# Pairing different half products on TensorE's two column tiles in the second matrix of an ELU block

## Chip, cores and metric

One Trainium2 chip, one core. The time is that of the device, in microseconds (us), the median of the runs shown. TensorE is called PE, VectorE DVE, ScalarE ACT, GpSimd POOL, as in the profile.

## What is computed

A sketched attention over q, k, v (4 batches, 4 heads, 1088 positions, 32 dimensions) gives an activation x of 4352 rows and 128 columns. An ELU block follows, and it is nearly all of the work:

```
h = x @ w_in                        # 128 -> 2048
g = where(h > 0, h, exp(min(h, 0)) - 1)
out = g @ w_out                     # 2048 -> 128, all float32
```

## The kernel before

The rows of x are worked through in groups of 512 (groups 0 to 7, and a group of 256 at the end). The 2048 columns of h are taken in eight steps of 256, two chunks of 128 partitions each. A step of a group has three parts. PE computes h for 512 rows (`mm1`, four passes of 512 columns per column tile, recorded at L256). ACT and DVE make g of it, chunk by chunk: RELU (L861) and EXP (L863) on ACT, one DVE operation (L869). Two steps later PE multiplies g with w_out (`mm2`).

The order on every engine is written out by hand in one loop: step n issues `mm1` of step n, its ELU, and then the `mm2` of step n-2.

In groups 2 to 7, and in the last two steps of group 1, `mm2` is done in seven half products instead of eight (`mm2_seven`, L770). The step's piece of w_out is a 2x2 of blocks (two chunks, two halves of 64 output features), and g is a 2x2 as well (two chunks, two halves of the 512 rows). Each product takes one 128x64 weight, a block of w_out or one of the sums in SS, and 256 columns, a block of g or one of the sums in tt. POOL makes the sums in tt for each step (`sums7`, L743: L751, then L753, then L754, each needing the one before). The products are called P1 to P7: P1, P2 and P3 need no sum from POOL, P5 and P7 need the result of L751, P6 that of L753 and P4 that of L754.

PE's 128 columns are used as two column tiles of 64 (four of 32 before step 30), each of which writes its own output partitions. Float32 makes two passes of each matrix multiplication. Before, each product runs on both tiles at once with the same weight: 128 of its 256 columns on tile 0 (partitions 0 to 63), the other 128 on tile 64 (partitions 64 to 127). So a step has 7 products x 2 passes of 128 columns on each tile. The products add up in two PSUM banks over the eight steps of a group: pa holds P1, P2, P6 and pb holds P4, P5, P7, P3, 128 columns each. There is one buffer of each, so the next group's first product into a bank waits until the closing additions have read it.

When a group's last `mm2` is through, its closing additions turn the seven sums into four output blocks. ACT copies P2 and P6 out of pa (`fin_seven_copy`, L801). DVE then adds twice from pa (`fin_seven_a`, L815, L816), does the ELU operation of the running step's second chunk, which POOL's next sums wait for, and only then adds three times from pb (`fin_seven_b`, L826 to L828), transposes (L830) and issues the 16 output transfers on the SP queue. In the loop the transposing part stands behind `sums7` of the step.

The 256 rows at the end (`mm1_last`, L903, and `mm2_last`, L924) follow group 7 in 16 short steps. They share four PSUM buffers named h, so `mm1_last` of short step 8 needs the DVE operation of short step 4 (L921) to be over. Group 7's closing additions stand between the DVE operations of short steps 2, 3 and 4.

Of the kernel before, what the change touches and what calls it, by code (L numbers as in the profile page):

```python
# [12 lines left out]
F32 = mybir.dt.float32  # L13
ALU = mybir.AluOpType
U32 = mybir.dt.uint32
MUL, ADD, SUB, MAX = ALU.mult, ALU.add, ALU.subtract, ALU.max
# [6 lines left out]
def _ap(ap: bass.AP, free):  # L23
    return dataclasses.replace(ap, ap=[list(ap.ap[0])] + [list(x) for x in free])
# [3 lines left out]
def kernel(  # L28
# [21 lines left out]
    nc = tc.nc  # L50
    B, H, S, D = q.shape
    R = S1.shape[0]
    P = 128
# [11 lines left out]
    work = ctx.enter_context(tc.tile_pool(name="wk", bufs=2))  # L65
# [91 lines left out]
    W = const.tile([P, NP, 4 * P], F32, name="W")  # L157
# [93 lines left out]
    width = [32]  # L251
# [244 lines left out]
    def half_tile(g, k):  # L496
        return (g // 2, 8 * (g % 2) + k) if g < NQ - 1 else (k, NT - 1)
# [242 lines left out]
    def quarter(g, cp, c, y):  # L740
        return gs[g, cp][:, c].rearrange("p (u x s) -> p u x s", u=2, x=2)[:, :, y, :]

    def sums7(g, cp, c):  # L743
        if c == 0:
            ts[g, cp] = work.tile([P, 4, 2, P], F32, name="tt", tag="raw", bufs=5)
        t = ts[g, cp]
        if c == 0:
            return
        b11, b21 = quarter(g, cp, 0, 0), quarter(g, cp, 1, 0)
        us = [[2 * P, 2], [1, P]]  # L750
        nc.gpsimd.tensor_tensor(_ap(t[:, 0], [[4 * P, 2], [P, 2], [1, P]]), _ap(gs[g, cp][:, 0, P:], [[4 * P, 2]] + us),  # L751
                                _ap(gs[g, cp][:, 0], [[P, 2]] + us), op=SUB)
        nc.gpsimd.tensor_tensor(t[:, 1], t[:, 2], b11, op=ADD)  # L753
        nc.gpsimd.tensor_tensor(t[:, 3], b21, t[:, 1], op=SUB)  # L754
# [13 lines left out]
                                         stop=False, skip_group_check=True, tile_position=(0, r))  # L768

    def mm2_seven(g, cp, first, last):  # L770
        if first and g == 1:
            acc[g].append(psum.tile([P, 512], F32, name="pa", tag="o0", bufs=1))
        elif first:
            acc[g] = [psum.tile([P, 512], F32, name="pa", tag="o0", bufs=1),
                      psum.tile([P, 512], F32, name="pb", tag="o1", bufs=1)]
        a, b = acc[g]
        t, w = ts.pop((g, cp)), [W[:, cp, 2 * P + 64 * i:2 * P + 64 * i + 64] for i in range(4)]
        b11, b21, b22 = quarter(g, cp, 0, 0), quarter(g, cp, 1, 0), quarter(g, cp, 1, 1)
        p1, p2, p6 = (a, 0, w[0], b11), (a, 1, w[2], b21), (a, 2, SS[:, 1, cp], t[:, 1])
        p4, p5 = (b, 0, w[3], t[:, 3]), (b, 1, SS[:, 0, cp], t[:, 0])  # L780
        p7, p3 = (b, 2, SS[:, 2, cp], t[:, 2]), (b, 3, SS[:, 3, cp], b22)
        if g == 1:
            p1, p2, p6, p3 = (b, 0) + p1[2:], (a, 0) + p2[2:], (b, 1) + p6[2:], (a, 1) + p3[2:]
            p5, p7, p4 = (b, 2) + p5[2:], (b, 3) + p7[2:], (a, 2) + p4[2:]
        todo = [p1, p2, p6, p3, p5, p7, p4] if first or last else [p1, p2, p3, p5, p7, p6, p4]
        for i, (bank, col, lhs, rhs) in enumerate(todo):
            for u in range(2):
                for w in range(0, 64, width[0]):
                    r = 64 * u + w
                    nc.tensor.matmul(bank[r:r + width[0], P * col:P * col + P], lhs[:, w:w + width[0]], rhs[:, u],  # L790
                                     start=(first and i in ((0,) if g == 1 else (0, 3))), stop=last, skip_group_check=True,
                                     tile_position=(0, r))
        del gs[g, cp]

    def fin_seven_copy(g):
        a = acc[g][0]
        sa = sas[g] = work.tile([P, 2, P], F32, name="sa", tag="sa", bufs=1)
        if g == 1:
            nc.scalar.copy(sa[:, 0], acc[g][1][:, :P])
            return  # L800
        nc.scalar.copy(sa[:].rearrange("p k s -> p (k s)"), a[:, P:3 * P])  # L801

    def fin_seven_a(g):
        a, sa = acc[g][0], sas.pop(g)
        uu = work.tile([P, 3, P], F32, name="uu", tag="uu", bufs=1)
        cc = work.tile([P, 4, P], F32, name="cc", tag="cc", bufs=1)
        sas[g] = uu, cc
        if g == 1:
            e = acc[g][1][:].rearrange("p (k s) -> p k s", s=P)
            nc.vector.tensor_tensor(uu[:, 0], sa[:, 0], e[:, 1], op=ADD)  # L810
            nc.vector.tensor_tensor(uu[:, 1:], _ap(uu[:, 0], [[0, 2], [1, P]]), e[:, 2:], op=ADD)
            nc.vector.tensor_tensor(cc[:, 3], uu[:, 2], e[:, 2], op=ADD)
            nc.vector.tensor_tensor(cc[:, 0], sa[:, 0], a[:, :P], op=ADD)
            return
        nc.vector.tensor_tensor(uu[:, 0], sa[:, 1], a[:, :P], op=ADD)  # L815
        nc.vector.tensor_tensor(cc[:, 0], sa[:, 0], a[:, :P], op=ADD)  # L816

    def fin_seven_b(g):
        b = acc.pop(g)[0 if g == 1 else 1]
        uu, cc = sas.pop(g)  # L820
        pb = b[:].rearrange("p (k s) -> p k s", s=P)
        if g == 1:
            nc.vector.tensor_tensor(cc[:, 1:3], uu[:, 1:], pb[:, 1:3], op=ADD)
            nc.vector.tensor_tensor(cc[:, 3], cc[:, 3], pb[:, 3], op=ADD)
        else:
            nc.vector.tensor_tensor(uu[:, 1:], _ap(uu[:, 0], [[0, 2], [1, P]]), pb[:, 1:3], op=ADD)  # L826
            nc.vector.tensor_tensor(cc[:, 2:], _ap(uu[:, 2], [[0, 2], [1, P]]), pb[:, 0:2], op=ADD)
            nc.vector.tensor_tensor(cc[:, 1], uu[:, 1], pb[:, 3], op=ADD)  # L828
        ob = work.tile([P, 2, 4, 2, D], F32, name="ob7", tag="ob", bufs=2)
        nc.vector.transpose(ob[:].rearrange("p h k w d -> p (h k w d)"), cc[:].rearrange("p k s -> p (k s)"))  # L830
        rows = out.rearrange("(b w y t) (e l d) -> b w e l y t d", b=B, w=2, t=NT, e=2, l=2)
        for u in range(2):
            bt, t = half_tile(g, 4 * u)
            for lo in range(2):
                r = slice(64 * u + 32 * lo, 64 * u + 32 * lo + 32)
                for hi in range(2):
                    for w in range(2):
                        nc.sync.dma_start(rows[bt, w, hi, lo, :, t:t + 4, :], ob[r, hi, :, w, :])

    def mm1(g, cp, cs=(0, 1)):  # L840
        n = qn[g] * P
# [266 lines left out]
    for n in range(2, N):  # L1108
        g, cp = steps[n]
        mm1(g, cp)  # L1110
        for f, *a in extra.get(n, ()):
            f(*a)
        if n == 30:
            width[0] = 64
        elu(g, cp, 0)
        if seven(g, cp):
            sums7(g, cp, 0)
        for f, *a in extra.get((n, 0), ()):
            f(*a)
        before = steps[n - 2]  # L1120
        ends = n > 3 and seven(*before) and before[1] == NP - 1
        if ends:
            elu_a(g, cp, 1, (0,))
            mm2_seven(*before, False, True)
            fin_seven_copy(before[0])
            elu_a(g, cp, 1, (1,))
            fin_seven_a(before[0])
            if before[0] == 1:
                fin_seven_b(1)
            elu_d(g, cp, 1)  # L1130
        else:
            elu(g, cp, 1)
        if seven(g, cp):
            sums7(g, cp, 1)
        if ends and before[0] > 1:
            fin_seven_b(before[0])
        for f, *a in extra.get((n, 1), ()):
            f(*a)
        g, cp = before
        if seven(g, cp):  # L1140
            if cp < NP - 1:
                mm2_seven(g, cp, cp == (NP - 2 if g == 1 else 0), False)
        elif g == 1:
            mm2_blocks(cp)
        elif n > 2:
            mm2(g, cp, cp == 0, cp == NP - 1)
            if cp == NP - 1:
                fin1(g)

    g = NQ - 2  # L1150
    for k in range(len(last) + lag):
        if k < lag:
            mm1_last(k)
            if k % 2:
                elu_last_a(k - 1)
                elu_last_d(k - 1)
                elu_last_a(k, (0,))
                mm2_seven(g, NP - 2 + k // 2, False, k == 3)
                if k == 3:
                    fin_seven_copy(g)  # L1160
                elu_last_a(k, (1,))
                if k == 3:
                    fin_seven_a(g)
                elu_last_d(k)
            if k == 3:
                fin_seven_b(g)
            continue
        if k < len(last):
            mm1_last(k)
            elu_last_a(k)  # L1170
            elu_last_d(k)
        mm2_last(k - lag)
        if last[k - lag][1] == NP - 1:
            fin_last(last[k - lag][0])
# [29 lines left out]
```

## Time and profile before

| what | value |
| --- | --- |
| median of 3 runs | 262.14 us (261.85 to 262.18) |
| span of the profiled execution | 260.6 us |
| PE busy | 254.8 us (98%) |
| DVE / ACT / POOL busy | 186.9 / 183.4 / 159.0 us |
| granted PE clock | 1.00 of full, 0.96 in the last 21 us |
| one step of groups 4 to 6 | 3.245 us |

The profiled execution has no time of its own beside its span; the median of the runs lies 1.5 us above that span. The 3.245 us come from two bursts of `mm2` ten steps apart, which begin at 188.79 and 221.24. A row of the timeline gives the start in us from the span's start, the duration in us, engine, line, operation, output and inputs, shape, and how many instructions it merges; brackets hold idle time and what ended it. Two tiles start a pass within some 0.01 us of each other, so "x8" of `mm2` is four passes on two tiles.

### The profile page before, as it was taken

The numbers are of one execution on the slowest core, as the hardware profiler recorded it, in microseconds if no ns is written. First come the engines' busy times: TensorE is split into PE (matmuls) and PEld (weight loads), VectorE is DVE, ScalarE is ACT, GpSimd is POOL, SyncE is SP. The second block draws the span as 40 slices with busy tenths as digits, with TensorE's granted clock in tenths as the row PEclk, the third lists the DMA queues.
The fourth block names the chain that finished last, engine by engine and source line by source line (L and its number), as shares of the span: only waits on it lengthen the run. The fifth ranks groups of instructions, "written<-read, shape, count | busy, mean of one in ns | idle before, by whom it ended". The sixth has DMA issues, their size and how long they took to land.

```text
span 260.6 us, 9756 instructions
## 1 busy us (share of the span) xinstructions
PE 254.8 (98%) x4123; PEld 158.4 (61%) x4123; DVE 186.9 (72%) x352; ACT 183.4 (70%) x358; POOL 159.0 (61%) x202
## 2 busy tenths in 40 slices
PE   8899999999999999999999999999999999999994
PEld 6753333453346667666666666665666666668993
DVE  6799999999988967997477675744466746544651
ACT  2379968766667577776687777775877777777792
POOL 3520007002179996788678798888688888887310
PEclk9999999999999999999999999999999999999999
DMA  5998079012112210002100204220001110110021
GB/s 173 330 358 222 3 223 268 24 21 85 28 18 28 31 34 18 3 15 34 20 0 4 33 10 104 60 30 13 3 3 27 34 26 3 25 19 3 3 30 33
DMA packets 30379, 15.61 MB, mean 60 GB/s; under 512 B 22496, under 2 KB 28000, under 8 KB 30336
## 3 DMA queue, kind: packets, MB, share of 16 engines
q1 hardware_dynamic: 29904, 14.63, 23.0%
q8 instruction: 32, 0.52, 0.9%
q10 hardware_dynamic: 368, 0.30, 0.3%
q0 software_dynamic: 64, 0.07, 0.1%
q14 instruction: 11, 0.09, 0.1%
HBM read 11.31 MB, written 2.36 MB: 52 GB/s over the span
## 4 chain that ended last, share of the span: by engine, by line
PE 97%; DVE 1%; ACT 0%; issue 0%; DVEq 0%
PE h L256 45%; PE pb L790 17%; PE pa L790 13%; PE o L256 5%; PE pb L766 4%; PE ol L256 3%; PE idle L264 1%; PE kv L435 1%; PE abp L343 1%; PE h L681 1%; PE h L551 1%; PE qtp L621 1%; DVE qp L609 1%; PE h L693 1%; PE xps L628 0%; PE kfps L365 0%
## 5 line engine op out<-in xcount | busy, mean ns | idle before, releaser
L256 PE MATMUL h<-xg,W 128*32 128x512 f32 (+3 forms) x904 | 130.8, 539 | 0.4 <-ACT xg L634 0.4
L869 DVE SCALAR_TENSOR_TENSOR gg<-e,h 128x512 f32<-128x512 f32 x128 | 85.9, 681 | 52.6 <-ACT e L863 47.8
L861 ACT ACTIVATE e<-h 128x512 f32<-128x512 f32 x128 | 75.5, 590 | 46.2 <-PE h L256 46.0
L863 ACT ACTIVATE e<-e 128x512 f32<-128x512 f32 x128 | 80.9, 632 | 3.8
L751 POOL TENSOR_TENSOR tt<-gg 128x512 f32<-128x512 f32 x50 | 64.3, 1286 | 28.9 <-DVE gg L869 25.2
L256 PEld LDWEIGHTS h<-xg,W 128*32 128x32 f32 (+1 forms) x904 | 43.0, 122 | 43.0 <-issue 34.4
L754 POOL TENSOR_TENSOR tt<-gg,tt 128x256 f32<-128x256 f32 x50 | 36.9, 739 | 3.9
L753 POOL TENSOR_TENSOR tt<-tt,gg 128x256 f32<-128x256 f32 x50 | 36.7, 734 | 3.9
L790 PEld LDWEIGHTS pa<-gg,W 128*64 128x64 f32 (+1 forms) x496 | 23.7, 126 | 22.4 <-issue 22.2
L790 PE MATMUL pa<-gg,W 128*64 128x128 f32 (+1 forms) x496 | 30.6, 274 | 0.0
L790 PE MATMUL pb<-tt,SS 128*64 128x128 f32 (+1 forms) x480 | 29.6, 273 | 0.0
L790 PEld LDWEIGHTS pb<-tt,SS 128*64 128x64 f32 (+1 forms) x480 | 22.8, 126 | 0.0
L790 PE MATMUL pa<-tt,SS 128*32 128x128 f32 (+1 forms) x288 | 21.2, 273 | 0.0
L790 PE MATMUL pb<-gg,SS 128*64 128x128 f32 (+1 forms) x256 | 19.9, 273 | 0.0
L790 PE MATMUL pb<-tt,W 128*64 128x128 f32 (+1 forms) x256 | 19.9, 273 | 0.0
L134 POOL TENSOR_TENSOR raw<-raw,tiny 128x512 f32<-128x512 f32 x1 | 1.0, 1041 | 24.7 <-DVE raw L129 24.7
L256 PE MATMUL o<-gg,W 128*32 128x512 f32 x128 | 15.3, 595 | 0.0
L790 PEld LDWEIGHTS pa<-tt,SS 128*32 128x32 f32 (+1 forms) x288 | 13.7, 124 | 0.0
L790 PEld LDWEIGHTS pb<-gg,SS 128*64 128x64 f32 (+1 forms) x256 | 12.8, 125 | 0.0
L790 PEld LDWEIGHTS pb<-tt,W 128*64 128x64 f32 (+1 forms) x256 | 12.8, 125 | 0.0
L766 PE MATMUL pb<-gg,W 128*32 128x256 f32 x192 | 11.5, 380 | 0.0
L921 DVE SCALAR_TENSOR_TENSOR gg<-e,h 128x256 f32<-128x256 f32 x16 | 6.6, 418 | 6.4 <-PE h L256 3.2
(163 smaller groups left out, 269.3 us busy)
## 6 DMA issues: line engine op xcount, KB each, us to landing
raw<-in_moe_w_in_dram SPq DMA_DIRECT2D x8, 256.0 KB, 6.3
raw<-in_moe_w_out_dram SPq DMA_DIRECT2D x8, 256.0 KB, 6.5
out_dram<-ob SPq DMA_DIRECT2D x112, 16.0 KB, 1.5
hd_k<-in_k_dram SPq DMA_DIRECT2D x3, 544.0 KB, 7.5
hd_q<-in_q_dram SPq DMA_DIRECT2D x3, 544.0 KB, 8.5
v<-in_v_dram SPq DMA_DIRECT2D x4, 288.0 KB, 7.1
v<-in_v_dram SPq DMA_DIRECT2D x4, 256.0 KB, 8.4
raw<-qpF SPq DMA_DIRECT2D x16, 64.0 KB, 2.0
```

The lines of the kernel that those rows point to most:

```text
L256: nc.tensor.matmul(dst[c:c + tile], lhs[:, c:c + tile], rhs, skip_group_check=True, tile_position=(0, c), **kw)
L264: nc.tensor.matmul(idle[c:c + tile, :cols], ones[:, :tile], ones[:, :cols], skip_group_check=True, tile_position=(0, c))
L343: nc.tensor.matmul(ps[i // 5][64 * u:64 * u + 64, 64 * (i % 5):64 * (i % 5) + 64], kT[b][:, u * KT + i, :], Sab[:].rearrange("p h y -> p ( ...
L751: nc.gpsimd.tensor_tensor(_ap(t[:, 0], [[4 * P, 2], [P, 2], [1, P]]), _ap(gs[g, cp][:, 0, P:], [[4 * P, 2]] + us), _ap(gs[g, cp][:, 0], [[ ...
L753: nc.gpsimd.tensor_tensor(t[:, 1], t[:, 2], b11, op=ADD)
L754: nc.gpsimd.tensor_tensor(t[:, 3], b21, t[:, 1], op=SUB)
L766: nc.tensor.matmul(acc[1][0][r:r + width[0], 256 * hi:256 * hi + 256], lhs[:, w:w + width[0]], gg[:, c, 256 * u:256 * u + 256], start=(cp ...
L790: nc.tensor.matmul(bank[r:r + width[0], P * col:P * col + P], lhs[:, w:w + width[0]], rhs[:, u], start=(first and i in ((0,) if g == 1 els ...
L861: nc.scalar.activation(e, hs[g, cp][c][:, :n], RELU, scale=-1.0)
L863: nc.scalar.activation(e, e, EXP, scale=-1.0)
L869: nc.vector.scalar_tensor_tensor(gs[g, cp][:, c, :n], es[g, cp][:, c, :n], -1.0, hs[g, cp][c][:, :n], op0=ADD, op1=MAX)
L921: nc.vector.scalar_tensor_tensor(gs["last", k // 2][:, k % 2, :2 * P], es["last", k // 2][:, k % 2, :2 * P], -1.0, hs["last", k][:, :2 * P ...
```

## The change

In groups 2 to 7 a product is no longer cut in two: it runs with all its 256 columns on one tile, and a different product runs on the other tile. P1 stands beside P6 and P5 beside P7 in bank pa, P3 beside P4 in bank pb. P2 alone is still cut in two halves of 128. The halves of g are now its first and its last 256 rows. Group 1 keeps the old form.

With that the sums come to lie on different partitions, and the closing additions change: the copy on ACT takes P1 and P6; DVE has seven additions instead of five, of which five work on 64 partitions only. All seven now stand ahead of the ELU operation of the second chunk (in group 7 four of them); the transpose and the output transfers stay behind it, in a function of their own. In a group's first and last step the pair P1 and P6 is first; in the others P2 is, then P5 with P7, P1 with P6, P3 with P4.

```diff
+        if g > 1:
+            gg, tt = gs[g, cp], t[:].rearrange("p k u s -> p k (u s)")
+            nc.gpsimd.tensor_tensor(_ap(tt[:, 0], [[4 * P, 2], [1, 2 * P]]), _ap(gg[:, 0, 2 * P:], [[4 * P, 2], [1, 2 * P]]),
+                                    _ap(gg[:, 0], [[2 * P, 2], [1, 2 * P]]), op=SUB)
+            nc.gpsimd.tensor_tensor(tt[:, 1], tt[:, 2], gg[:, 0, :2 * P], op=ADD)
+            nc.gpsimd.tensor_tensor(tt[:, 3], gg[:, 1, :2 * P], tt[:, 1], op=SUB)
+            return
...
+        one_six = (a, 0, ((w[0], b11), (SS[:, 1, cp], t[:, 1])), first)
+        five_seven = (a, 256, ((SS[:, 0, cp], t[:, 0]), (SS[:, 2, cp], t[:, 2])), False)
+        three_four = (b, 0, ((SS[:, 3, cp], b22), (w[3], t[:, 3])), first)
+        two = (b, 256, ((w[2], b21[:, :P]), (w[2], b21[:, P:])), False)
+        todo = [one_six, five_seven, three_four, two] if first or last else [two, five_seven, one_six, three_four]
+        for bank, col, both, start in todo:
+            for v in range(0, 64, width[0]):
+                for u, (lhs, rhs) in enumerate(both):
+                    r = 64 * u + v
+                    nc.tensor.matmul(bank[r:r + width[0], col:col + rhs.shape[1]], lhs[:, v:v + width[0]], rhs,
+                                     start=start, stop=last, skip_group_check=True, tile_position=(0, r))
...
+        nc.scalar.copy(sa[:], acc[g][0][:, :2 * P])
...
+        for u in range(2):
+            nc.vector.tensor_tensor(u2[64 * u:64 * u + 64], sa[64:], a[:64, :256], op=ADD)
+        nc.vector.tensor_tensor(u2, u2, a[:, 256:], op=ADD)
+        nc.vector.tensor_tensor(c2[64:, 256:], u2[64:], a[:64, 256:], op=ADD)
...
+        nc.vector.tensor_tensor(c2[:, :256], u2, b[:, :256], op=ADD)
+        for u in range(2):
+            nc.vector.tensor_tensor(c2[:64, 256 + P * u:256 + P * u + P], sa[:64, P * u:P * u + P],
+                                    b[64 * u:64 * u + 64, 256:256 + P], op=ADD)
...
             fin_seven_a(before[0])
-            if before[0] == 1:
-                fin_seven_b(1)
+            fin_seven_b(before[0])
             elu_d(g, cp, 1)
...
-        if ends and before[0] > 1:
-            fin_seven_b(before[0])
+        if ends:
+            fin_seven_out(before[0])
```

The seven additions are called V1 to V7 below, in the order of the diff: V1 and V2 in the first loop, V3, V4, then V5, and V6 and V7 in the last loop.

More of the change, by code (lines that the diff above doesn't have):

```diff
@@ L770, in mm2_seven @@
     def mm2_seven(g, cp, first, last):
-        if first and g == 1:
-            acc[g].append(psum.tile([P, 512], F32, name="pa", tag="o0", bufs=1))
-        elif first:
+        if g == 1:
+            mm2_seven_blocks(cp, first, last)
+            return
+        if first:
             acc[g] = [psum.tile([P, 512], F32, name="pa", tag="o0", bufs=1),
@@ L776, in mm2_seven @@
         a, b = acc[g]
+        gg, t = gs.pop((g, cp)), ts.pop((g, cp))[:].rearrange("p k u s -> p k (u s)")
+        w = [W[:, cp, 2 * P + 64 * i:2 * P + 64 * i + 64] for i in range(4)]
+        b11, b21, b22 = gg[:, 0, :256], gg[:, 1, :256], gg[:, 1, 256:]
+        one_six = (a, 0, ((w[0], b11), (SS[:, 1, cp], t[:, 1])), first)
+        five_seven = (a, 256, ((SS[:, 0, cp], t[:, 0]), (SS[:, 2, cp], t[:, 2])), False)
+        three_four = (b, 0, ((SS[:, 3, cp], b22), (w[3], t[:, 3])), first)
+        two = (b, 256, ((w[2], b21[:, :P]), (w[2], b21[:, P:])), False)
@@ L777, in mm2_seven, with mm2_seven_blocks @@
+    def mm2_seven_blocks(cp, first, last):
+        g = 1
+        if first:
+            acc[g].append(psum.tile([P, 512], F32, name="pa", tag="o0", bufs=1))
+        a, b = acc[g]
         t, w = ts.pop((g, cp)), [W[:, cp, 2 * P + 64 * i:2 * P + 64 * i + 64] for i in range(4)]
         b11, b21, b22 = quarter(g, cp, 0, 0), quarter(g, cp, 1, 0), quarter(g, cp, 1, 1)
-        p1, p2, p6 = (a, 0, w[0], b11), (a, 1, w[2], b21), (a, 2, SS[:, 1, cp], t[:, 1])
-        p4, p5 = (b, 0, w[3], t[:, 3]), (b, 1, SS[:, 0, cp], t[:, 0])
@@ L781, in mm2_seven @@
[L781 to L785, printed above, removed]
+        todo = [(b, 0, w[0], b11), (a, 0, w[2], b21), (b, 1, SS[:, 1, cp], t[:, 1]), (a, 1, SS[:, 3, cp], b22),
+                (b, 2, SS[:, 0, cp], t[:, 0]), (b, 3, SS[:, 2, cp], t[:, 2]), (a, 2, w[3], t[:, 3])]
@@ L786, in mm2_seven @@
         for i, (bank, col, lhs, rhs) in enumerate(todo):
             for u in range(2):
[L788 to L792, printed above, removed]
+                for v in range(0, 64, width[0]):
+                    r = 64 * u + v
+                    nc.tensor.matmul(bank[r:r + width[0], P * col:P * col + P], lhs[:, v:v + width[0]], rhs[:, u],
+                                     start=(first and i == 0), stop=last, skip_group_check=True, tile_position=(0, r))
@@ L793, in mm2_seven @@
         del gs[g, cp]
     def fin_seven_copy(g):
-        a = acc[g][0]
-        sa = sas[g] = work.tile([P, 2, P], F32, name="sa", tag="sa", bufs=1)
+        sa = sas[g] = work.tile([P, 2 * P], F32, name="sa", tag="sa", bufs=1)
         if g == 1:
-            nc.scalar.copy(sa[:, 0], acc[g][1][:, :P])
+            nc.scalar.copy(sa[:, :P], acc[g][1][:, :P])
             return
-        nc.scalar.copy(sa[:].rearrange("p k s -> p (k s)"), a[:, P:3 * P])
+        nc.scalar.copy(sa[:], acc[g][0][:, :2 * P])
@@ L806, in fin_seven_a @@
         cc = work.tile([P, 4, P], F32, name="cc", tag="cc", bufs=1)
-        sas[g] = uu, cc
+        sas[g] = sa, uu, cc
         if g == 1:
             e = acc[g][1][:].rearrange("p (k s) -> p k s", s=P)
-            nc.vector.tensor_tensor(uu[:, 0], sa[:, 0], e[:, 1], op=ADD)
+            nc.vector.tensor_tensor(uu[:, 0], sa[:, :P], e[:, 1], op=ADD)
             nc.vector.tensor_tensor(uu[:, 1:], _ap(uu[:, 0], [[0, 2], [1, P]]), e[:, 2:], op=ADD)
             nc.vector.tensor_tensor(cc[:, 3], uu[:, 2], e[:, 2], op=ADD)
-            nc.vector.tensor_tensor(cc[:, 0], sa[:, 0], a[:, :P], op=ADD)
+            nc.vector.tensor_tensor(cc[:, 0], sa[:, :P], a[:, :P], op=ADD)
@@ L814, in fin_seven_a @@
             return
-        nc.vector.tensor_tensor(uu[:, 0], sa[:, 1], a[:, :P], op=ADD)
-        nc.vector.tensor_tensor(cc[:, 0], sa[:, 0], a[:, :P], op=ADD)
+        u2, c2 = uu[:, :2].rearrange("p k s -> p (k s)"), cc[:].rearrange("p k s -> p (k s)")
+        for u in range(2):
+            nc.vector.tensor_tensor(u2[64 * u:64 * u + 64], sa[64:], a[:64, :256], op=ADD)
+        nc.vector.tensor_tensor(u2, u2, a[:, 256:], op=ADD)
+        nc.vector.tensor_tensor(c2[64:, 256:], u2[64:], a[:64, 256:], op=ADD)
@@ L818, in fin_seven_b @@
     def fin_seven_b(g):
         b = acc.pop(g)[0 if g == 1 else 1]
-        uu, cc = sas.pop(g)
-        pb = b[:].rearrange("p (k s) -> p k s", s=P)
+        sa, uu, cc = sas.pop(g)
+        sas[g] = cc
         if g == 1:
+            pb = b[:].rearrange("p (k s) -> p k s", s=P)
             nc.vector.tensor_tensor(cc[:, 1:3], uu[:, 1:], pb[:, 1:3], op=ADD)
             nc.vector.tensor_tensor(cc[:, 3], cc[:, 3], pb[:, 3], op=ADD)
[L825 to L828, printed above, removed]
+            return
@@ L829, in fin_seven_b, with fin_seven_out @@
+        u2, c2 = uu[:, :2].rearrange("p k s -> p (k s)"), cc[:].rearrange("p k s -> p (k s)")
+        nc.vector.tensor_tensor(c2[:, :256], u2, b[:, :256], op=ADD)
+        for u in range(2):
+            nc.vector.tensor_tensor(c2[:64, 256 + P * u:256 + P * u + P], sa[:64, P * u:P * u + P],
+                                    b[64 * u:64 * u + 64, 256:256 + P], op=ADD)
+    def fin_seven_out(g):
+        cc = sas.pop(g)
         ob = work.tile([P, 2, 4, 2, D], F32, name="ob7", tag="ob", bufs=2)
@@ L832, in fin_seven_b @@
         for u in range(2):
-            bt, t = half_tile(g, 4 * u)
             for lo in range(2):
                 r = slice(64 * u + 32 * lo, 64 * u + 32 * lo + 32)
-                for hi in range(2):
+                for i in range(2):
+                    hi, y = (i, u) if g == 1 else ((0, 1), (1, 0), (0, 0), (1, 1))[2 * i + u]
+                    bt, t = half_tile(g, 4 * y)
                     for w in range(2):
-                        nc.sync.dma_start(rows[bt, w, hi, lo, :, t:t + 4, :], ob[r, hi, :, w, :])
+                        nc.sync.dma_start(rows[bt, w, hi, lo, :, t:t + 4, :], ob[r, i, :, w, :])
     def mm1(g, cp, cs=(0, 1)):
@@ L1166 @@
                 fin_seven_b(g)
+                fin_seven_out(g)
             continue
```

## Prediction, before the changed kernel was run

> **What bounds the kernel now.** I read the page first: who is busy, and the chain that ended last.
>
> ```profile
> PE 254.8 (98%) x4123; PEld 158.4 (61%) x4123; DVE 186.9 (72%) x352; ACT 183.4 (70%) x358; POOL 159.0 (61%) x202
> ...
> PE 97%; DVE 1%; ACT 0%; issue 0%; DVEq 0%
> ```
>
> PE is busy 98% of the span and is 97% of the chain. So two questions decide: what the changed passes cost PE, and whether something new makes PE wait. For the first, PE's timeline of a step (the last of group 4 ends at 166.00):
>
> ```profile
> 166.00 1.89 PE L256 MATMUL h<-xg,W 128*64 128x512 f32 x8
> 167.72 0.61 PE L790 MATMUL pa<-gg,W 128*64 128x128 f32 x8
> 168.15 0.39 PE L790 MATMUL pa<-tt,SS 128*64 128x128 f32 x4
> ```
>
> Starts, not durations, tell the pace: eight passes in pairs take 168.15 - 167.72. The shapes are separated best over long stretches. The 256-row tail has passes of 128 columns alone: from 244.47 to 254.08 it does 11 short steps of 8 slots, 0.1092 us per slot (a slot is one pass on all tiles). A step of 3.245 us holds 14 of these and four of 512 columns, which leaves 0.429 each. The two give 0.000833 us per column and 0.0026 us fixed. A slot of 256 columns should then take 0.2158; the row below shows eight in 43.15 - 41.42, 0.216.
>
> ```profile
> 41.42 1.91 PE L766 MATMUL pb<-gg,W 128*32 128x256 f32 x32
> 43.15 1.04 PE L256 MATMUL h<-xg,W 128*32 128x512 f32 x8
> ```
>
> So weight loads are hidden even at 128 columns, and PE is within 3% of its column count. For the second question I read DVE around the end of group 4, then POOL there:
>
> ```profile
> 165.18 0.69 DVE L869 SCALAR_TENSOR_TENSOR gg<-e,h 128x512 f32<-128x512 f32 x1 [1.47 <-ACT e L863]
> 165.87 0.29 DVE L815 TENSOR_TENSOR uu<-sa,pa 128x128 f32<-128x128 f32 x1
> 166.07 0.28 DVE L816 TENSOR_TENSOR cc<-sa,pa 128x128 f32<-128x128 f32 x1
> 166.40 0.69 DVE L869 SCALAR_TENSOR_TENSOR gg<-e,h 128x512 f32<-128x512 f32 x1
> 167.00 0.42 DVE L826 TENSOR_TENSOR uu<-uu,pb 128x256 f32<-128x256 f32 x1
> 167.46 0.42 DVE L827 TENSOR_TENSOR cc<-uu,pb 128x256 f32<-128x256 f32 x1
> 167.79 0.28 DVE L828 TENSOR_TENSOR cc<-uu,pb 128x128 f32<-128x128 f32 x1
> 168.11 0.71 DVE L830 STREAM_TRANSPOSE ob<-cc 128x512 f32<-128x512 f32 x1
> ```
>
> ```profile
> 167.23 1.28 POOL L751 TENSOR_TENSOR tt<-gg 128x512 f32<-128x512 f32 x1 [0.54 <-DVE gg L869]
> 168.59 0.73 POOL L753 TENSOR_TENSOR tt<-tt,gg 128x256 f32<-128x256 f32 x1
> 169.39 0.73 POOL L754 TENSOR_TENSOR tt<-gg,tt 128x256 f32<-128x256 f32 x1
> ```
>
> The reader is to see two spacings on DVE. L828 starts 0.33 after L827, before that has ended: they do not depend on each other. L827 starts 0.46 after L826, whose result it reads: after its end. For 128 columns the two are 0.20 (L815 to L816) and 0.32 (L828 to L830). And POOL's sums start 0.83 after the second ELU operation starts (166.40) and end 2.89 later, at 170.12; their burst of mm2 begins at 170.96. PE has 0.84 us to spare there.
>
> **PE's own work.** Per step 12 slots of 128 columns become 6 of 256; the columns stay the same. That saves 6 x 0.0026 = 0.0155 us, in 48 steps **0.75 us**. Two different products side by side cost nothing extra: the four heads of L435 (own weight and own columns on each of four tiles) start within 0.02 us of each other.
>
> **POOL, transfers, ACT.** POOL's three sums keep their sizes (1.28, 0.73, 0.73), and SP's 16 transfers per group stay. The new order needs the sums earlier: L751's after 0.22 us of the burst instead of 0.65, L753's after 0.65 instead of 1.09, L754's after 1.08 instead of 1.31; P6 at once in first and last steps. In the steady steps L753 ends 1.8 us and L754 1.0 us before the burst, so nothing is due. In group 7's last step L753 ends at 242.80 and the burst begins at 242.94: with 0.1 us for the load that waits, **0.05 us**. The copy on ACT waited for P2 and P6; now it waits for the whole bank, P5 and P7 included. Their last pass starts at 164.47 + 3 x 0.216 = 165.12 and takes 0.38 (L766's row): the copy starts at 165.55, not 165.48, and V1 at 165.95.
>
> **The closing additions, groups 3 to 6.** All seven now precede the ELU operation. Operations on 64 partitions are in no row, so I take the 128-partition durations (0.42, 0.28) and ask only for the spacing. V3 needs V1 and V2, V4 needs V3: 0.46 twice. V5 to V6 stays on the same partitions: 0.33. V1 to V2, V4 to V5, V6 to V7 and V7 to the ELU operation change from one half of the partitions to the other. Lower end, overlapped: 0.33 + 0.33 + 0.20 + 0.20, in all 2.31 us. Upper end, each after the other's end: 0.46 + 0.46 + 0.32 + 0.32, in all 2.81. I take the upper one, because every overlapped pair in the trace starts on the same partition in all operands, and these do not; the pairs it shows without overlap are those where the second is not free to start.
>
> [...]
>
> Then the ELU operation starts at 165.95 + 2.81 = 168.76 instead of 166.40. POOL's third sum ends at 168.76 + 0.83 + 2.89 = 172.48. A load that waits starts some 0.04 after (L754 of the last step ends at 243.61, DVE's waiting L921 starts at 243.65), and a pass whose load could not run ahead loses 0.09 (the slots at the changes of tile shape, as 180.27 to 180.80, take 0.52 instead of 0.43): P4 at 172.61. PE would be there at 170.96 - 0.03 + 1.08 = 172.01. **0.60 us late**; lower end 0.10. Bank pa, too: V4 ends at 165.95 + 1.38 + 0.42 = 167.75, the next group's first pass was due at 167.70; 0.2 us late, but within the 0.60, since POOL's time does not move with it. Four ends: **2.4 us** (0.4). What else is late next has cover: mm1 two steps on needs the ELU result at 170.1. Group 2's end has 0.65 us more of PE work (L435) ahead of either burst, and costs nothing; its DVE queue, full until 118, is 1 us later, and POOL still ends 0.7 us ahead of need.
>
> **The end of group 7.** The copy starts at 244.06 (now 243.82), V1 at 244.46. V4 starts 1.38 later; then the ELU operation of short step 3 (+0.46), V5 (+0.33), V6 (+0.33), V7 (+0.32), the transpose (+0.32), and the ELU of short step 4 (+0.71) at 248.31:
>
> ```profile
> 246.06 0.71 DVE L830 STREAM_TRANSPOSE ob<-cc 128x512 f32<-128x512 f32 x1
> 246.69 0.71 DVE L921 SCALAR_TENSOR_TENSOR gg<-e,h 128x256 f32<-128x256 f32 x2
> ...
> 247.97 0.61 PE L256 MATMUL h<-xg,W 128*64 128x128 f32 x8
> ```
>
> It is 246.69 now. The pass at 247.97 is mm1 of short step 8, which waits for that result's buffer: 248.31 + 0.42 + 0.13 = 248.86, **0.85 us late** (lower end 0.43). After it PE is dense to the end, so the loss stays.
>
> **The sum** against the profiled execution (260.6): -0.75 + 0.05 + 2.4 + 0.85 = +2.55, so 263.1; the median lies 1.5 above, **264.6**. With the lower ends: +0.13, 262.3.
>
> **Rivals.** About 0.2% (0.5 us) is what a measurement can tell from no change.
> 1. Overlap: DVE runs the half-partition operations into each other. Only 0.4 + 0.43 + 0.05 us are lost and PE's gain nearly pays: 262.3. For it: durations on DVE go by columns; against: no such pair is shown. Chance 0.22.
> 2. No wait at all: the buffers come free in time and PE's gain stands alone: 262.14 - 0.75 = 261.4, faster. It decides if V1 to V7 take under some 2.2 us and the tail's transpose finds 0.4 us. Against: V1 to V4 alone need 1.25. Chance 0.08.
> 3. The pair does not run side by side but in turns: 3 pairs x 2 passes x 0.216 x 48 = +62 us. Against: L435. Chance 0.02.
> My forecast has the rest, 0.68, and a range of its own of 263.8 to 265.2 (spacing of the held pairs 0.42 instead of 0.46 takes 0.15 off each end; 0.1 us more per held load adds 0.5).
>
> **Chances and range.** Faster 0.08, same 0.22, slower 0.70. The range takes in most of rival 1: 262.0 to 265.3.
>
> **What would show it.** Right: mm2 slots at 0.216; V1 to V2 0.42 or more apart; after the ends of groups 3 to 6 PE waiting for POOL's L754 sum in the new group's second step; a gap of 0.8 us ahead of short step 8. Wrong: overlapping additions, or passes of different products that do not start together.

## The result, and the profile after

| | kernel before | changed kernel |
| --- | --- | --- |
| median of 5 runs each, one after the other | 261.85 us (261.73 to 262.18) | 264.07 us (263.79 to 264.16) |
| span of the profiled execution | 260.6 us | 262.1 us |
| from the first mm1 burst to PE's last end ("PE's stretch") | 240.62 us | 242.68 us |
| from PE's last end to the end of the span | 3.70 us | 3.71 us |

The changed kernel is slower by a ratio of 1.0079 (95% interval 1.0067 to 1.0091), 2.2 us. PE's stretch, from the first pass of mm1 in group 0 to the end of PE's last matmul, is the sharpest measure here: what lies ahead of it, loading and the attention, varied between executions (the first burst begins at 16.2 us before and at 15.7 after, though no code there differs; in one run below at 17.7). It grew by 2.06 us.

The page's busy lines and chain of the changed kernel, by themselves, hardly show it:

```profile
PE 255.7 (98%) x3403; PEld 151.9 (58%) x3403; DVE 191.9 (73%) x364; ACT 183.7 (70%) x358; POOL 158.2 (60%) x202
...
PE 96%; DVE 1%; ACT 0%; issue 0%; DVEq 0%
```

PE has 720 matmuls fewer and still 98%. The stages tell more. The DVE timeline of the changed kernel at group 4's end, where V1 and V2 are L838, V3 L839, V4 L840, V5 L852, V6 and V7 L854, the ELU operation L900:

```profile
165.59 0.84 DVE L838 TENSOR_TENSOR uu<-sa,pa 64x256 f32<-64x256 f32 x2
166.47 0.42 DVE L839 TENSOR_TENSOR uu<-uu,pa 128x256 f32<-128x256 f32 x1
166.93 0.42 DVE L840 TENSOR_TENSOR cc<-uu,pa 64x256 f32<-64x256 f32 x1
167.38 0.42 DVE L852 TENSOR_TENSOR cc<-uu,pb 128x256 f32<-128x256 f32 x1
167.71 0.58 DVE L854 TENSOR_TENSOR cc<-sa,pb 64x128 f32<-64x128 f32 x2
168.32 0.69 DVE L900 SCALAR_TENSOR_TENSOR gg<-e,h 128x512 f32<-128x512 f32 x1
```

From V1 to the ELU operation 2.73 us pass; it was 0.53. V1 and V2 together take 0.84, twice 0.42: the second starts when the first has ended. POOL's sums, which need that ELU result, come late in proportion, and PE waits for the third of them with P4 (pb<-tt,W), while P3 on the other tile (pb<-gg,SS) goes ahead:

```profile
169.15 1.28 POOL L751 TENSOR_TENSOR tt<-gg 128x512 f32<-128x512 f32 x1 [2.81 <-DVE gg L900]
170.51 0.73 POOL L753 TENSOR_TENSOR tt<-tt,gg 128x256 f32<-128x256 f32 x1
171.32 0.73 POOL L754 TENSOR_TENSOR tt<-gg,tt 128x256 f32<-128x256 f32 x1
```

```profile
171.91 0.38 PE L797 MATMUL pb<-gg,SS 128*64 128x256 f32 x1
172.10 0.43 PE L797 MATMUL pb<-tt,W 128*64 128x256 f32 x1
```

The sum ends at 172.05, and P4 starts 0.19 us behind P3, which in other steps it accompanies. Earlier in the same end two banks are late, too. These are the next group's first passes into them on the second tile, which is the later of the two:

```profile
167.50 0.43 PE L797 MATMUL pa<-tt,SS 128*64 128x256 f32 x1
168.44 0.43 PE L797 MATMUL pb<-tt,W 128*64 128x256 f32 x1
```

The one into pa starts 0.57 us after the pass of 512 columns ahead of it, at 167.50 instead of 167.36: V4, the last reader of pa, ended at 167.35. The one into pb is 0.03 us late: V7, the last reader of pb, ended at 168.29. Behind each of the three late passes the next one comes late by 0.05 us more (it starts 0.27 us after it instead of 0.216). So of the loss at this end some 0.19 us arise at bank pa, 0.08 at bank pb and 0.21 at the third sum.

The other place is short step 8. PE's timeline, then DVE's:

```profile
248.28 0.61 PE L256 MATMUL ol<-W,gg 128*64 128x128 f32 x8
249.47 0.66 PE L256 MATMUL h<-xg,W 128*64 128x128 f32 x8 [0.59 <-DVE gg L952]
```

```profile
248.26 0.71 DVE L860 STREAM_TRANSPOSE ob<-cc 128x512 f32<-128x512 f32 x1
249.00 1.41 DVE L952 SCALAR_TENSOR_TENSOR gg<-e,h 128x256 f32<-128x256 f32 x4
```

The ELU operation of short step 4 starts at 249.00, behind all the additions and the transpose; PE's pass that needs its buffer at 249.47. The four slots ahead (x8 on two tiles) should end at 248.28 + 4 x 0.109 = 248.72; the stop is 0.75, with 0.05 behind it 0.80.

### The profile page after: what moved, and what is told of

It reads as the page before. It is cut to its first block, busy times and chain, and to the rows that moved or that the text cites. A ratio compares the mean times of both kernels' runs of the same rounds, so it can differ in the third digit from the quotient of the medians.

```text
span 262.1 us, 8325 instructions
## 1 busy us (share of the span) xinstructions
PE 255.7 (98%) x3403; PEld 151.9 (58%) x3403; DVE 191.9 (73%) x364; ACT 183.7 (70%) x358; POOL 158.2 (60%) x202
## 4 chain that ended last, share of the span: by engine, by line
PE 96%; DVE 1%; ACT 0%; issue 0%; DVEq 0%
PE h L256 46%; PE pa L797 16%; PE pb L797 12%; PE o L256 5%; PE pb L773 4%; PE ol L256 3%; PE idle L264 1%; PE kv L435 1%; PE h L681 1%; PE abp L343 1%; PE pa L813 1%; PE h L551 1%; PE qtp L621 1%; PE h L693 0%; PE pb L813 0%; DVE qp L609 0%
## 5 line engine op out<-in xcount | busy, mean ns | idle before, releaser
L256 PE MATMUL h<-xg,W 128*32 128x512 f32 (+3 forms) x904 | 135.8, 540 | 1.0 <-DVE gg L952 0.6
L900 DVE SCALAR_TENSOR_TENSOR gg<-e,h 128x512 f32<-128x512 f32 x128 | 85.5, 680 | 49.6 <-ACT e L894 48.3
L256 PEld LDWEIGHTS h<-xg,W 128*32 128x32 f32 (+1 forms) x904 | 53.1, 122 | 43.6 <-issue 24.4
L751 POOL TENSOR_TENSOR tt<-gg 128x512 f32<-128x512 f32 x48 | 62.1, 1294 | 22.6 <-DVE gg L900 20.1
L797 PE MATMUL pa<-tt,SS 128*64 128x256 f32 (+1 forms) x360 | 53.6, 380 | 0.0
L753 POOL TENSOR_TENSOR tt<-tt,gg 128x256 f32<-128x256 f32 x48 | 35.2, 734 | 3.8
L754 POOL TENSOR_TENSOR tt<-gg,tt 128x256 f32<-128x256 f32 x48 | 35.1, 732 | 3.8
L797 PEld LDWEIGHTS pa<-tt,SS 128*64 128x64 f32 (+1 forms) x360 | 29.0, 126 | 1.6
L797 PE MATMUL pb<-tt,W 128*64 128x256 f32 (+1 forms) x120 | 29.3, 382 | 0.0
L797 PE MATMUL pa<-gg,W 128*64 128x256 f32 (+1 forms) x120 | 28.9, 380 | 0.0
L797 PE MATMUL pb<-gg,SS 128*64 128x256 f32 (+1 forms) x120 | 28.9, 380 | 0.0
L797 PEld LDWEIGHTS pb<-gg,W 128*64 128x64 f32 (+1 forms) x240 | 17.5, 126 | 12.1 <-issue 7.8
L797 PE MATMUL pb<-gg,W 128*64 128x128 f32 (+1 forms) x240 | 23.4, 274 | 0.0
L797 PEld LDWEIGHTS pa<-gg,W 128*64 128x64 f32 (+1 forms) x120 | 12.5, 126 | 8.6 <-ACT e L892 3.3
```

The lines of the kernel that those rows point to most:

```text
L256: nc.tensor.matmul(dst[c:c + tile], lhs[:, c:c + tile], rhs, skip_group_check=True, tile_position=(0, c), **kw)
L751: nc.gpsimd.tensor_tensor(_ap(tt[:, 0], [[4 * P, 2], [1, 2 * P]]), _ap(gg[:, 0, 2 * P:], [[4 * P, 2], [1, 2 * P]]), _ap(gg[:, 0], [[2 * P, ...
L753: nc.gpsimd.tensor_tensor(tt[:, 1], tt[:, 2], gg[:, 0, :2 * P], op=ADD)
L754: nc.gpsimd.tensor_tensor(tt[:, 3], gg[:, 1, :2 * P], tt[:, 1], op=SUB)
L797: nc.tensor.matmul(bank[r:r + width[0], col:col + rhs.shape[1]], lhs[:, v:v + width[0]], rhs, start=start, stop=last, skip_group_check=Tru ...
L900: nc.vector.scalar_tensor_tensor(gs[g, cp][:, c, :n], es[g, cp][:, c, :n], -1.0, hs[g, cp][c][:, :n], op0=ADD, op1=MAX)
```

## Experiments

The theory: additions on half of the partitions are held until the one ahead has ended (V1 and V2, 0.84 us for twice 0.42), all seven stand ahead of the ELU operation, and so POOL's sums and bank pa are late at four ends, and a buffer at the tail. Rivals: the number of additions, not the holding (A); the pairing or the new order on PE (B). Each run was timed beside the kernel before, whose median was 261.86 to 262.04 us. The table gives the ratio to it; "behind PE" is the time from PE's last end to the span's end.

| run | median us | ratio (95% interval) | PE's stretch | behind PE |
| --- | --- | --- | --- | --- |
| full partitions | 262.59 | 1.0029 (1.0013 to 1.0045) | 240.71 | 3.71 |
| old closing | 261.45 | 0.9983 (0.9973 to 0.9993) | 239.91 | 3.70 |
| old products | 264.10 | 1.0082 (1.0069 to 1.0095) | 242.79 | 3.71 |
| tail spread | 265.82 | 1.0146 (1.0133 to 1.0159) | 241.88 | 6.18 |
| P2 by ACT | 262.73 | 1.0036 (1.0024 to 1.0048) | 241.21 | 4.91 |
| V5 to V7 behind | 266.05 | 1.0154 (1.0140 to 1.0167) | 244.51 | 3.71 |
| transpose late | 264.02 | 1.0073 (1.0060 to 1.0086) | 241.95 | 4.73 |
| late and split | 263.14 | 1.0049 (1.0036 to 1.0062) | 241.94 | 3.70 |
| all mended | 262.59 | 1.0026 (1.0013 to 1.0038) | 240.71 | 4.16 |
| mended, split | 265.79 | 1.0152 (1.0138 to 1.0165) | 244.20 | 3.70 |
| POOL additions | 262.34 | 1.0011 (1.0000 to 1.0022) | 240.86 | 3.82 |
| POOL early | 261.33 | 0.9986 (0.9968 to 1.0004) | 239.92 | 3.83 |

### Full partitions

The first four runs take the change apart: the halves of the partitions, the closing, the products, the tail.

```diff
-        for u in range(2):
-            nc.vector.tensor_tensor(u2[64 * u:64 * u + 64], sa[64:], a[:64, :256], op=ADD)
+        nc.vector.tensor_tensor(u2, sa[:], a[:, :256], op=ADD)
+        nc.vector.tensor_tensor(w2, sa[:], a[:, :256], op=ADD)
...
```

V3, V4, V6 and V7 are changed likewise.

> The seven additions keep their places, columns and order of dependence, but each works on all 128 partitions, so none changes from one half to the other (the second addition writes a buffer of its own, and the sums come out as other sums than the reference's). Theory (the half-partition additions are held until the one ahead has ended, and what they lose sets POOL's sums, bank pa and the buffer of short step 8): the first addition to the ELU operation takes 2.31 us instead of 2.73, so PE's wait for POOL's third sum (0.19 us at each of four ends) and most of the wait for bank pa (0.14) go, some 4 x 0.3 = 1.2, and the 0.80 us at the tail shrinks by 0.4: 1.6 us less than the changed kernel's 264.1, about 262.4. Rival A (the spacing is the same on all partitions; only the number of additions ahead of the ELU operation counts): 264.1. Rival B (the loss is in the products on PE): 264.1.

Measured: 262.59 us; PE's stretch is 2.0 us shorter than the changed kernel's. The DVE timeline of this run at group 4's end, V1 (L838) to the ELU operation (L900):

```profile
167.19 0.42 DVE L838 TENSOR_TENSOR uu<-sa,pa 128x256 f32<-128x256 f32 x1
167.53 0.41 DVE L839 TENSOR_TENSOR uu<-sa,pa 128x256 f32<-128x256 f32 x1
167.98 0.42 DVE L840 TENSOR_TENSOR uu<-uu,pa 128x256 f32<-128x256 f32 x1
168.43 0.42 DVE L841 TENSOR_TENSOR uu<-uu,pa 128x256 f32<-128x256 f32 x1
168.77 0.41 DVE L853 TENSOR_TENSOR cc<-uu,pb 128x256 f32<-128x256 f32 x1
169.10 0.48 DVE L855 TENSOR_TENSOR cc<-sa,pb 128x128 f32<-128x128 f32 x2
169.50 0.68 DVE L900 SCALAR_TENSOR_TENSOR gg<-e,h 128x512 f32<-128x512 f32 x1
```

Twice the elements, and yet 2.31 us instead of 2.73. Where the changed kernel goes from one half of the partitions to the other the second operation here starts before the first has ended: V1 to V2 0.34 instead of 0.43, V4 to V5 0.34 instead of 0.45, V6 to V7 0.20 instead of 0.29, V7 to the ELU operation 0.20 instead of 0.32. So these four are held in the changed kernel, where the second starts 0.01 to 0.03 us after the first has ended, and overlap here. The width of 64 partitions alone did not hold an operation: V6, on 64 partitions, starts 0.33 us after V5, on 128, in the changed kernel too, before V5 has ended, and both begin at partition 0. Rivals A and B fall: the wait for the third sum is gone, that for pa costs 0.11 us at each end and the one at the tail 0.36. Of the rise to 262.59 over the kernel before, PE's stretch explains 0.1 alone; in the profiled execution the first burst began at 17.7 us, and what made it late is not shown.

### Old closing, old products

```diff
-            fin_seven_b(before[0])
+            if before[0] == 1:
+                fin_seven_b(1)
             elu_d(g, cp, 1)
...
```

The new products, with the five additions of the kernel before:

> The products of the change, paired on column tiles in their new order, with the five closing additions of the kernel before in their old places, two of them ahead of the ELU operation, all on 128 partitions (one of them reads the third quarter of bank pb where the old one read the fourth, which is not written; the outputs are other sums than the reference's). Theory: PE's gain stands alone, 0.7 to 0.75 us under the kernel before: 261.1 to 261.2 where that is at 261.9, with no wait at the four ends or at short step 8. Rival B (pairs of different products, or their new order, lose time on PE themselves): at or above the kernel before; 263 or more if all of the loss is theirs.

Measured: PE's stretch is 0.71 us shorter than before, no burst is late at any end or at short step 8. The pairing costs PE nothing: each of the 48 steps is 0.0148 us shorter. The opposite half, the old `mm2_seven` with the new closing:

> The other half of the change alone: the products of the kernel before in their old order, with the seven closing additions of the change (two of them read columns 128 to 384 of bank pa in place of columns 256 to 512, whose last quarter is not written; the outputs are other sums than the reference's). Theory: the whole loss without the gain: 4 x 0.48 + 0.80 = 2.7 us over the kernel before, 264.6; up to 0.5 us less, since the sums are due later in the old order (the third 1.31 us into its burst instead of 1.08). Rival B: 261.9, as before.

Measured: 264.10 us, PE's stretch 2.17 us longer than before: 0.40 at each of the four ends, where P3 waits 0.24 us for bank pb, and 0.58 at short step 8. The two halves alone make -0.71 + 2.17 = 1.46 us, together 2.06, so with the new products the same additions are dearer by 0.6 us. That the new order wants the sums earlier and lets the copy start later fits this; no run takes the two apart.

### P2 by ACT, V5 to V7 behind the ELU operation

```diff
+            for u in range(2):
+                nc.scalar.copy(s2[g][:64, P * u:P * u + P], acc[g][1][64 * u:64 * u + 64, 256:256 + P])
...
+            nc.vector.tensor_tensor(cc[:].rearrange("p k s -> p (k s)")[:64, 256:], sa[:64], s2.pop(g)[:64], op=ADD)
```

The last line stands for V6 and V7, behind the ELU operation and just ahead of the transpose.

> The change, but ScalarE copies P2 out of bank pb (two copies of 64x128, behind its EXP), so that bank pb is free without V6 and V7, and the two become one addition of 64x256 from SBUF behind the ELU operation, just ahead of the transpose. V1 to V5 stay ahead of the ELU operation. Theory: the ELU operation and POOL's sums come 0.6 us earlier at the four ends, PE's wait for the third sum (0.19) and what follows from it go, the wait for bank pa (0.14) stays; at the tail short step 4's ELU operation is 0.17 earlier: 264.1 - 4 x 0.34 - 0.17 = 262.5. Rival (bank pa alone sets the loss, POOL's sums only come to stand beside it): 263.9 or more.

Measured: 262.73 us; at each end 0.20 us are left, all of it at bank pa, and P4 goes beside P3 again. Since ACT's copy frees bank pb early as well, the 0.29 us that are gone from each end are the third sum's and pb's together; the trace of the changed kernel has 0.21 and 0.08 for them. The profiled execution of this run ended 4.91 us behind PE, although SP issued the last output 0.34 us after PE's end. Its span was 261.8 us, those of the other eight executions 260.6 to 260.8; what delayed that one transfer stays open.

> The change, but V5, V6 and V7 are issued behind the ELU operation, where the kernel before had them; V1 to V4 stay ahead of it. The ELU operation starts 0.94 us earlier, so the wait for POOL's third sum goes at the four ends. But V7 ends at about 0.6 us past the moment when the next group's third pass wants bank pb. Theory (whichever of bank pa, bank pb and the sums is free last sets the loss): 0.14 + 0.58 instead of 0.48 at each of four ends, the tail as in the changed kernel: 264.1 + 1.0 = 265.1. Rival (the ELU operation's delay is what costs): 264.1 - 1.3 = 262.8.

Measured: 266.05 us. The sums are early, but P3 waits 0.63 us for V7 to leave bank pb; an end costs 0.88 us, and group 2's end 0.26. Moving the additions only chose another late resource; the theory's place was right, its size 0.16 too small per end, and it had left out group 2's.

### Tail spread, transpose late, late and split

```diff
         if k < len(last):
             mm1_last(k)
             elu_last_a(k)
             elu_last_d(k)
+        if k - lag < len(closing):
+            closing[k - lag](g)
```

> The change, but the closing additions of group 7 (and the transpose) are not issued together in short step 3: one follows the ELU operation of each short step from 4 on. Theory: the buffer of short step 8 is free in time, and the 0.80 us at that place go; nothing else moves: 263.3. Rival (PE's stop there has another cause, or the additions make later short steps wait instead): 264.1, with the wait at another short step.

Measured: 265.82 us, 1.75 slower than the changed kernel and not 0.8 faster. PE did gain what was expected: its stretch is 0.80 us shorter, and no short step waits. But the span ends 6.18 us behind PE. SP's queue in this run:

```profile
253.10 7.57 SPq L869 DMA_DIRECT2D out_dram<-ob  x16
260.77 0.55 SPq L1010 DMA_DIRECT2D out_dram<-ol  x1
```

SP issues group 7's 16 transfers one after the other, and the last output's transfer, ready when PE is through at 257.6, stands behind them. A transfer queue became the bound, and the theory had not considered it. So I moved the transpose alone, and less far:

```diff
                 fin_seven_b(g)
-                fin_seven_out(g)
...
+        if k == 5:
+            fin_seven_out(NQ - 2)
```

> The change, but group 7's transpose and its 16 transfers are issued behind the ELU operation of short step 5 and not of short step 3; the seven additions stay. In the run with the closing spread over the short steps PE lost nothing at short step 8, and the end came 3.6 us after it instead of at PE's pace, since SP's 16 issues (about 8 us) began at 253.1 and the last output's transfer stands behind them. Here the transpose starts at about 249.1: short step 4's ELU operation comes 0.7 us earlier, and SP is through with the 16 at about 257.8, when the last output is ready. Theory: -0.75 against the changed kernel, 263.3; up to 0.4 more if SP's issues end later. Rival (the seven additions themselves, not the transpose, hold short step 8): 264.1.

Measured: PE's stretch 0.73 us shorter, as expected; with the transpose out of the way the seven additions hold short step 8 by 0.07 us only. But SP's 16 issues took 9.65 us this time and ended at 259.48; the time is 264.02.

```profile
249.83 9.65 SPq L869 DMA_DIRECT2D out_dram<-ob  x16
259.59 0.55 SPq L974 DMA_DIRECT2D out_dram<-ol  x1
```

The third run gives eight of the 16 to POOL's queue:

```diff
+                        eng = nc.gpsimd if g == NQ - 2 and w else nc.sync
+                        eng.dma_start(rows[bt, w, hi, lo, :, t:t + 4, :], ob[r, i, :, w, :])
```

> As the run with the late transpose, but GpSimd's queue issues eight of group 7's 16 transfers. Theory (PE's gain of 0.73 us at the tail was lost to SP, whose 16 issues ended at 259.48 with the last output's issue behind them): the time from PE's end to the span's end falls from 4.7 us to 3.7, and the time is 263.3. Rival (the end hangs on the transfers themselves, however issued): 264.0.

Measured: 263.14 us, 3.70 behind PE. SP's queue:

```profile
249.63 4.73 SPq L870 DMA_DIRECT2D out_dram<-ob  x8
258.00 0.55 SPq L975 DMA_DIRECT2D out_dram<-ol  x1
```

The last output is issued 0.34 us after PE's end (257.66). So in the run with the late transpose it was SP's queue, and not the transfers themselves, that ended the span late.

### Mended versions

All mended: ACT swaps the halves as it copies, so that V1 and V2 become one addition on 128 partitions; P2 by ACT; the transpose late.

```diff
+            nc.scalar.copy(sa[64 * u:64 * u + 64], acc[g][0][64 - 64 * u:128 - 64 * u, :2 * P])
...
+        nc.vector.tensor_tensor(u2, sa[:], a[:, :256], op=ADD)
```

> The change with all that was learnt: ScalarE swaps the halves while it copies P1 and P6 out (two copies of 64x256), so that V1 and V2 become one addition on 128 partitions; ScalarE copies P2 out, so that V6 and V7 become one addition from SBUF behind the ELU operation; group 7's transpose follows short step 5's ELU operation. Theory: PE's gain of 0.71 is left, less some 0.05 at each of four ends for bank pa (the two copies cost about what the one addition saves): 262.1 - 0.5 = 261.4 where the kernel before takes 261.9. Rival (ScalarE's four copies delay its own RELU and EXP, or V1 by over 0.5 us): 262.3 or more, with a wait of PE for bank pa.

Measured: 262.59 us. Half of the rival held: DVE idles 0.51 us ahead of V1 until ACT's second copy is through, where V1 came 0.08 us after the ELU operation ahead of it in the changed kernel (165.51 to 165.59). So V1 starts 0.43 us later, which is what V2 saves, and pa still costs 0.20 us at each end. And SP's issues end late again (4.16 behind PE). Next, P5 is copied too (the addition that reads it, V4, moves behind the ELU operation), and the queues are split:

```diff
+            n = 2 * P + 2 * P * u
+            nc.scalar.copy(sa[64 * u:64 * u + 64, :n], acc[g][0][64 - 64 * u:128 - 64 * u, :n])
...
-        nc.vector.tensor_tensor(c2[64:, 256:], u2[64:], a[:64, 256:], op=ADD)
...
+            nc.vector.tensor_tensor(c2[64:, 256:], uu[:, :2].rearrange("p k s -> p (k s)")[64:], sa[64:, 256:], op=ADD)
```

> As the run with all mended, with two more edits. ScalarE's second copy takes P5 too (64x512 instead of 64x256, some 0.2 us more), so that the addition that reads P5 is from SBUF and goes behind the ELU operation, and bank pa is free after the addition ahead of it, 0.25 us earlier. And of group 7's 16 transfers GpSimd's queue issues eight, so that SP reaches the last output in time. Theory: the wait of 0.14 us at each of four ends goes, and the time from PE's end to the span's end is 3.7 us again (4.2 in the run with all mended): PE's stretch from its first mm1 burst to its end 240.2 us (240.62 in the kernel before), the time 261.5 where the kernel before takes 261.95. Rival (these waits come back elsewhere, or GpSimd's eight issues end later than SP's sixteen did): 262.3 or more.

Measured: 265.79 us; the expectation failed by 4.3 us. No end waits for pa, but DVE and POOL at group 5's end show something new, V4 (L869) and P1 + P2 (L870), both with two inputs from SBUF:

```profile
198.31 0.42 DVE L869 TENSOR_TENSOR cc<-uu,sa 64x256 f32<-64x256 f32 x1
198.75 1.41 DVE L870 TENSOR_TENSOR cc<-sa,s 64x256 f32<-64x256 f32 x1
```

```profile
198.43 1.45 POOL L751 TENSOR_TENSOR tt<-gg 128x512 f32<-128x512 f32 x1 [2.24 <-DVE gg L913]
```

and in group 7's tail, with POOL idle:

```profile
250.71 0.42 DVE L869 TENSOR_TENSOR cc<-uu,sa 64x256 f32<-64x256 f32 x1
251.14 0.42 DVE L870 TENSOR_TENSOR cc<-sa,s 64x256 f32<-64x256 f32 x1
```

The addition that starts behind POOL's L751 lasts 1.41 us and ends 0.28 after L751 does (199.88); the one that starts ahead of it lasts 0.42, and L751 then takes 1.45 instead of 1.28. So it is at all five ends in the loop (L870's six additions take 1.246 us on the mean). In the kernel before, L827, with one input from PSUM, also starts behind an L751 (167.46, L751 from 167.23 to 168.51), and takes 0.42. I call the long addition blocked by L751; that is read from these durations, and what holds it is not shown. DVE's queue is 1 us late behind it; at group 2's end, where DVE has no slack, PE loses 1.0 us, and from group 3's end on the two tiles run out of step. The test gives the two additions to POOL, which is idle there:

```diff
-            nc.vector.tensor_tensor(c2[64:, 256:], uu[:, :2].rearrange("p k s -> p (k s)")[64:], sa[64:, 256:], op=ADD)
-            nc.vector.tensor_tensor(c2[:64, 256:], sa[64:, :256], s2.pop(g)[64:], op=ADD)
+        nc.gpsimd.tensor_tensor(c2[64:, 256:], u2[64:], sa[64:, 256:], op=ADD)
+        nc.gpsimd.tensor_tensor(c2[:64, 256:], sa[64:, :256], s2.pop(g)[64:], op=ADD)
```

> As the run with all mended and split queues, but the two additions whose inputs both come from SBUF are GpSimd's, ahead of its sums for the next step (64x256 each), and not VectorE's behind the ELU operation. In that run VectorE's second such addition took 1.41 us at each of the five ends inside the loop, where GpSimd's L751 was running when it was to start, and 0.42 at the tail, where GpSimd was idle; from the group 3 end on the sums came late and PE's two column tiles ran out of step, 3.5 us in all. GpSimd idles 2.8 us ahead of L751 there. Theory (the blocked addition is the cause): PE's stretch from its first mm1 burst to its end is 240.2 us, the time 261.5 where the kernel before takes 261.95. Rival (the longer copy on ScalarE, or another of the edits, is the cause): 265.8 as before, or over 262.3 at least; a second rival: GpSimd's additions delay L751 by over 0.4 us and PE waits for the third sum again, 262.5.

Measured: 262.34 us. With both additions off DVE, PE's stretch is 3.3 us shorter. The move takes the 0.84 us that the two last when not blocked off DVE as well. But the run with all mended has one such addition in the same place, ahead of L751 (168.25, L751 from 168.36) and not blocked (0.42 us), and there PE loses nothing at group 2's end; the blocked addition is the likely cause. The second rival is there too: L751 waits until 168.66 for POOL's own additions, and P4 is 0.18 us late. So the last run has ACT copy P2 ahead of its EXP, and POOL add P1 + P2 first:

```diff
+            fin_seven_copy_2(before[0])
             elu_a(g, cp, 1, (1,))
-            fin_seven_copy_2(before[0])
```

> As the run with GpSimd's two additions, but ScalarE copies P2 ahead of its EXP and not behind it, and GpSimd does P1 + P2 first and the addition of P5 second: the first can start at 166.55 in group 4's end, the second at 167.3 and end at 168.03, ahead of the 168.37 at which the ELU result lets L751 start (in the run before they ended at 168.58, L751 started at 168.66, and the fourth product's pass at 171.62 was 0.18 us late). The EXP ends at 167.15, still ahead of the ELU operation at 167.53. Theory: no wait of PE is left at the four ends, PE's stretch from its first mm1 burst to its end is 240.0 to 240.2 us, and the time 261.4 to 261.6 where the kernel before takes 261.95. Rival (the two column tiles out of step, or the EXP that is moved, cost the difference): 262.3 as in the run before.

Measured: 261.33 us, ratio 0.9986, PE's stretch 239.92, as with the old closing. POOL at group 4's end:

```profile
166.47 0.72 POOL L847 TENSOR_TENSOR cc<-sa,s 64x256 f32<-64x256 f32 x1 [0.43 <-ACT s L832]
167.27 0.73 POOL L864 TENSOR_TENSOR cc<-uu,sa 64x256 f32<-64x256 f32 x1
168.12 1.29 POOL L751 TENSOR_TENSOR tt<-gg 128x512 f32<-128x512 f32 x1
```

Both additions are over before L751 can start, and no end loses time. The earlier copy has a second effect: in the two runs ahead V5 started 0.32 us late, behind ACT's copies of P2 (L832), and here it does not. So a version with the paired products keeps 0.70 us of PE's gain. Its spans were 259.4 to 259.7 us in eight executions, those of the kernel before 260.0 to 260.5 in twelve; two of its eight times (262.17 and 263.11) lie above the rest, and by the interval of the times alone it isn't told from the kernel before.

## Why the prediction was right, and where its sizes were off

The time came out 0.5 us under the forecast (264.07 for 264.6) and inside the forecast's own range, by the waits that it named: PE waiting for L754's sum after the four ends, and a stop of 0.8 us ahead of short step 8.

- **PE's gain**, 0.75: measured 0.71 (0.0148 per step), shown by the run with the old closing. That run also answers the rival of passes in turns.
- **P6 in group 7's last step**, 0.05: nothing. L753 ends 0.12 us ahead of the pass.
- **The held additions.** The upper end, 2.81, was chosen, as an estimate: no row of the kernel before had an operation on 64 partitions. Measured 2.73 (the held pairs 0.43 to 0.45 and 0.29 to 0.32 apart, not 0.46 and 0.32). The lower end, 2.31, is what the run on full partitions took. So rival 1's premise was wrong, while its time (262.3) is about what that run shows.
- **Four ends of 0.60**: 0.49 each, (2.06 + 0.71 - 0.80) / 4. The mis-sized terms are the chain (0.08 too long) and the load that waits: P4 starts 0.05 after the sum's end and loses 0.05 more behind it, 0.10 in all for 0.13. The prediction booked the whole loss under the sum, with bank pa's wait inside it, and did not name bank pb. The total does hang on the sum, which comes last, but PE loses it in three places: some 0.19 at pa, 0.08 at pb, 0.21 at the sum. So a mend of the sum alone can't win it all: the run with P2 by ACT, which frees the sum and pb, keeps 0.20 at pa. And with the sums early, bank pb can take their place (V5 to V7 behind).
- **The tail**, 0.85: 0.80. (The forecast's two moments, 247.97 and 248.86, lie 0.89 apart; the step from there to 0.85 is not written out.) The queue of DVE operations ahead of that ELU operation was too long by this much, and it helps to take any of them away: the transpose moved behind two more ELU operations gave 0.73 back with all seven additions in place, and additions that overlap gave 0.45 (full partitions).
- **Group 2's end** costs nothing, as said: the bursts on both sides of it keep their pace.
- **The time outside the stretch.** The sum was +2.55 for a span of 263.1. The span is 262.1: PE's stretch grew by 0.5 us less, and the first burst of the profiled execution came 0.5 us earlier. On the other side the median lies 1.9 us above that span and not 1.5. That the last two nearly cancel is luck.
- Not foreseen, since the change itself does not touch it: SP's 16 issues have only some 1.4 us to spare ahead of the last output (257.36 to 258.76 in the changed kernel).

## What to carry to other kernels

Count the operations that stand ahead of the one result that another engine waits for, and price those that change their half of the partitions at the full duration of the one ahead: of 256 columns they started 0.43 and 0.45 us apart here, on full partitions 0.34, and fewer elements cost more time (2.73 us against 2.31). When a wait is mended, ask what is late next, in the issue queues too: the sums, a PSUM bank, the transfer queue and an L751 running on POOL each took over in turn here. A saving of 0.3% on the bound engine is kept only if the closing work finds an idle engine and an idle moment.

## What the runs showed of the hardware that I had not expected

- A VectorE addition of 64x256 with both inputs in SBUF that started while POOL's L751 was running took 1.41 us, at five ends of the run mended and split; at its tail, with POOL idle, 0.42.
- ACT's copies of 64x256 and of 64x512 (L826, six each) took 0.473 us on the mean in the run mended and split. In the changed kernel those of 128x256 take 0.37 and of 128x512 (L622) 0.59, 0.48 on the mean: half of the partitions saved nothing.
- PE's first pass into a bank started 0.15 us after VectorE's last read of it had ended (167.35 to 167.50, 168.29 to 168.44), but 0.05 us after the end of GpSimd's sum (172.05 to 172.10).
- After a wait on one column tile alone, the two tiles kept the offset in the changed kernel: P3's passes run some 0.2 us ahead of P4's (171.91 and 172.10, 172.12 and 172.37), and the burst behind them starts in two halves (172.34 and 172.58). In the run mended and split the tiles drifted apart from group 3's end on.
- SP's 16 issues of the same transfers took 7.6 to 9.7 us in different executions; what sets this stays open.
